# Reciprocal root mean square of blocks 1 to 8 on VectorE alone, in a fused attention and two-layer kernel

## The chip, the cores and the metric

The kernel runs on one core of a Trainium2 chip. The metric is the device time of one execution in microseconds; a lower time is better. Five engines of the core matter here: PE (TensorE, matrix products, with PEld for its weight loads), ACT (ScalarE), DVE (VectorE), POOL (GpSimd) and SP (SyncE, which only issues transfers). Each works through its own list of instructions in order, and they wait for each other through semaphores.

## The reference, cut to what matters

```python
x = attention(q, k, v)                      # chunks of 64, then 4608 rows of 512
rms = np.sqrt(np.mean(x * x, axis=-1, keepdims=True) + 1e-06)
xn = x / rms * rms_g
g = xn @ w_gate
silu = g * (1.0 / (1.0 + np.exp(-g)))
x = (silu * (xn @ w_val)) @ w_out           # 512 -> 1536 -> 512
h = x @ w_in                                # 512 -> 2048
y = (h * np.clip(h + 3.0, 0.0, 6.0) / 6.0) @ w_out2
```

The change touches the second line: one over `rms` for each of the 4608 rows.

## The kernel before

The 4608 rows are worked in nine blocks of 512. A block lies with its 512 features across partitions (four tiles of 128) and its 512 rows along the free dimension. Block 0 is normalised in a start-up stage that the change leaves alone. Then PE runs the first layer: blocks 0 to 2 one after the other (a gate product, a value product and a down product for each of twelve pieces, lines L1023 and L1048 to L1051), then blocks 3 to 8 in pairs with a scheme of seven products for eight (`product`, L1034). The second layer follows in the last half and has none of the changed code.

While PE works on the matrices of one block, the attention of later blocks and their normalisation are slipped in between. An agenda holds, for each tick (two or three slots of matrix products), the steps that are issued then: `at(t, fn, turn=...)`, and inside a tick the steps go by their turn. Each engine keeps the order in which its instructions were issued. So the place of a step is set by the agenda, and an engine that waits for a step holds up all that stands behind it.

The class `Rms` does the normalisation of blocks 1 to 8, one object for each block, in five steps of turn 1:

- `halve` (L957, L958) splits the 128 x 512 sums of squares in two parts;
- `mean` (L962, L963) multiplies both by a matrix of ones into bank `ATT` of the PSUM tensor `PS`, so that all 128 partitions hold the sum of squares of each row; ScalarE then takes the square root (L965) into the SBUF tile `rt`;
- `inv` transposes `rt` by 32 x 32 blocks on VectorE (L970), so that 16 columns hold the 512 values, takes the reciprocal of those 16 columns (L971), and transposes back with a broadcast (L972);
- `norm` (L984), in two halves, multiplies the block by the gains and by `rt`.

The banks `ATT` and `ATT + 1` are also those of attention: `Pair` (blocks 2 to 4) and `Wide` (blocks 5 to 8) write their scores there (L799 and L928), read the maxima (L809, L939), transpose the probabilities (L837) and form the values (L855). Whoever writes bank `ATT` next has to wait until the sums of squares have been read from it. The agenda places the steps of blocks 5 and 7 so that `mean` comes in tick 30, and in tick 31 `inv` (turn 1) and right after it the first half of the scores of the next unit (turn 2).

Square root, SiLU (L1331, L1353) and exponential (L709, L818) need different tables on ScalarE: each change of function from one to another has an ACT_TABLE_LOAD ahead of it, which the compiler puts in. Copies, casts, squares and ReLU need none.

Other names that come up: `ah` (L1077) and `al` (L1079 on GpSimd) are the two parts of a gated activation, which the down product L1048 to L1051 reads; L1357 and L1358 are the same for the paired blocks; L1362 is VectorE's multiply or add of a product that leaves PSUM; L1444 is a ScalarE copy of such a product.

Of the kernel before, what the change touches and what calls it, by code (L numbers as in the profile page):

```python
# [10 lines left out]
F32 = mybir.dt.float32  # L11
F32R = mybir.dt.float32r
U32 = mybir.dt.uint32
AF = mybir.ActivationFunctionType
ALU = mybir.AluOpType
# [59 lines left out]
def fused_kernel(  # L75
# [13 lines left out]
    nc = tc.nc  # L89
    B, H, S, D = q.shape  # L90
    NT, DM = out.shape
# [4 lines left out]
    N = 512  # L96
# [3 lines left out]
    scale = 1.0 / float(D) ** 0.5  # L100
# [3 lines left out]
    few_p = ctx.enter_context(tc.tile_pool(name="few", bufs=2))  # L104
# [8 lines left out]
    at_p = ctx.enter_context(tc.tile_pool(name="at", bufs=1))  # L113
# [7 lines left out]
    eps = const.tile([128, 1], F32, name="eps")  # L121
# [362 lines left out]
    sqs = {}  # L484
# [16 lines left out]
    class Att:  # L501
# [117 lines left out]
        def mean(self):  # L619
            self.ms = PS[:, self.bank, 0:1]  # L620
            for a in range(KD):
                nc.tensor.matmul(
                    self.ms, self.sq[:, a * 128:(a + 1) * 128], ones[:, 0:1], start=a == 0, stop=a == KD - 1
                )
# [9 lines left out]
        def inv(self):  # L634
            nc.vector.reciprocal(self.r, self.r)
            self.dg = self.sq[:, 384:512]
            nc.vector.tensor_scalar(self.dg, ident, self.r, None, op0=ALU.mult)
# [310 lines left out]
    class Rms:  # L948
# [11 lines left out]
        def mean(self):  # L960
            ps = PS[:, ATT, :]
            nc.tensor.matmul(ps, ones_r, self.hl[:, 0, :], start=True, stop=False)  # L962
            nc.tensor.matmul(ps, ones_r, self.hl[:, 1, :], start=False, stop=True)  # L963
            self.rt = at_p.tile([128, N], F32, tag="sqs", name="rt")
            nc.scalar.activation(self.rt, ps, AF.Sqrt, scale=1.0 / DM, bias=eps)  # L965

        def inv(self):
            t = at_p.tile([128, N], F32, tag="p", name="rT")
            r = few_p.tile([128, 16], F32, tag="rc", name="rc")
            nc.vector.transpose(out=t, in_=self.rt)  # L970
            nc.vector.reciprocal(r, t.rearrange("p (j n) -> p j n", n=32)[:, :, 0])  # L971
            nc.vector.transpose(  # L972
                out=self.rt.rearrange("p (j n) -> p j n", n=32),
                in_=r.rearrange("p (j o) -> p j o", o=1).to_broadcast([128, 16, 32]),
            )
# [140 lines left out]
    with tc.manual_schedule():  # L1116
# [208 lines left out]
        for b in range(3):  # L1325
            prev, late = None, None
            hk = 0
            for f in range(FA):
                mm_up(GB, whole(W["gate", f]), xs)
                s = sg_p.tile([128, N], F32, tag="sg", name="sg")  # L1330
# [33 lines left out]
        for p in range(3):  # L1364
# [4 lines left out]
            def gt(f, z):  # L1369
                key = ("x", 0) if z == 0 and f < 4 else (z, f // 2)  # L1370
                if key not in g:
                    g[key] = (
                        xn_p.tile([128, KD, N], F32, tag="XL", name="ge")
                        if key == ("x", 0)
                        else wp.tile([128, 2, N], F32, tag="w", name="gu")
                    )
                return g[key][:, f % 4 if key == ("x", 0) else f % 2, :]
# [6 lines left out]
            for i in range(NI + 1):  # L1384
# [13 lines left out]
                for n, (pr, m) in enumerate(slots):  # L1398
# [19 lines left out]
                    elif (pr, m) == (3, 0):  # L1418
                        t = gt(h0, 1)
                        vec(t, t, bank(4, 0), ALU.add)  # L1420
                        later = t
                    elif (pr, m) == (4, 1):
                        t = gt(h1, 0)
# [3 lines left out]
                    elif (pr, m) == (3, 1):  # L1427
                        s = hold.pop("s2")
                        vec(s, s, bank(4, 1), ALU.add)
                        t = gt(h0, 1)  # L1430
# [8 lines left out]
                    elif (pr, m) == (2, 1):  # L1439
                        t = gt(f0, 0)  # L1440
                        vec(t, t, bank(0, 1), ALU.mult)
                    elif (pr, m) == (7, 0):
                        t = gt(f1, 1)
# [3 lines left out]
                    elif (pr, m) == (7, 1):  # L1447
# [3 lines left out]
                        t = gt(f1, 1)  # L1451
# [70 lines left out]
        for n, f in enumerate(fs):  # L1522
            bank = 6 + n % 2
            i, m, z = f // 4, f // 2 % 2, f % 2
# [5 lines left out]
            s = sg_p.tile([128, N], F32, tag="sg", name="sg")  # L1530
# [24 lines left out]
        def slot(i, name):  # L1555

            key = (i, name)
            if key not in G:
                if i < 2 and name != "t":
                    t = xn_p.tile([128, KD, N], F32, tag=("XH", "XL")[i], name="gx")  # L1560
                    names = ("11", "12", "21", "22")
                elif name == "t":
                    t = wp.tile([128, 2, N], F32, tag="w", name="gt")
                    names = ()
                else:
                    t = wp.tile([128, 2, N], F32, tag="w", name="gu")
                    names = ("11", "12") if name[0] == "1" else ("21", "22")
                for n, x in enumerate(names):
                    G[i, x] = t[:, n, :]
                if not names:  # L1570
                    for n in range(2):
                        G[i - i % 2 + n, "t"] = t[:, n, :]
            return G[key]
# [81 lines left out]
        for b in range(1, NB, 2):  # L1655
# [7 lines left out]
            for I in range(NG + 1):  # L1663
# [7 lines left out]
                for pr, m in slots:  # L1671
# [20 lines left out]
                    elif pr == 3:  # L1692
                        t = slot(i, "12")
# [7 lines left out]
                    elif pr == 7:  # L1701
                        t = slot(i, "22")
# [124 lines left out]
```

## Time and profile before

| what | value |
|---|---|
| time before, median of 3 runs | 1680.77 us (1678.62 to 1683.74) |
| time of the profiled execution | 1679.51 us |
| its span, first to last instruction | 1677.7 us |
| granted TensorE clock, mean | 0.995 |
| PE busy | 1649.2 us (98%) |
| DVE busy | 1086.8 us (65%) |
| ACT busy | 845.2 us (50%) |
| POOL busy | 459.5 us (27%) |

The profiled execution took 1.8 us more than its span, which lies before the first and after the last instruction, and 1.26 us less than the median. Busy shares are shares of the span. Matrix products are pipelined, so a busy PE may still run more slowly than it could; the idle time before an instruction, and what ended it, is the safer reading.

### The profile page before, as it was taken

The numbers are of one execution on the slowest core, as the hardware profiler recorded it, in microseconds if no ns is written. First come the engines' busy times: TensorE is split into PE (matmuls) and PEld (weight loads), VectorE is DVE, ScalarE is ACT, GpSimd is POOL, SyncE is SP. The second block draws the span as 40 slices with busy tenths as digits, with TensorE's granted clock in tenths as the row PEclk, the third lists the DMA queues.
The fourth block names the chain that finished last, engine by engine and source line by source line (L and its number), as shares of the span: only waits on it lengthen the run. The fifth ranks groups of instructions, "written<-read, shape, count | busy, mean of one in ns | idle before, by whom it ended". The sixth has DMA issues, their size and how long they took to land.

```text
span 1677.7 us, 26541 instructions
## 1 busy us (share of the span) xinstructions
PE 1649.2 (98%) x9920; PEld 1350.7 (81%) x9920; DVE 1086.8 (65%) x1600; ACT 845.2 (50%) x1409; POOL 459.5 (27%) x336
## 2 busy tenths in 40 slices
PE   8999999999999999999999999999999999999998
PEld 7777888878878888788887888888788878887886
DVE  6998566656575775758436378448746764874475
ACT  6786344455454454645434344455445544654552
POOL 1001434321326522364226622131023003301310
PEclk8999999999999999999999999999999999999999
DMA  9913777747876488855979766667767786777665
GB/s 301 271 37 71 207 208 222 205 152 251 292 262 224 168 297 286 290 176 185 361 238 316 293 239 226 213 190 250 219 209 224 209 243 191 223 218 235 189 200 150
DMA packets 336096, 375.07 MB, mean 224 GB/s; under 512 B 184288, under 2 KB 260064, under 8 KB 335840
## 3 DMA queue, kind: packets, MB, share of 16 engines
q1 hardware_dynamic: 273984, 302.84, 58.4%
q10 hardware_dynamic: 61984, 70.53, 12.2%
q8 instruction: 79, 1.29, 0.3%
q14 instruction: 49, 0.40, 0.1%
HBM read 292.55 MB, written 80.74 MB: 223 GB/s over the span
## 4 chain that ended last, share of the span: by engine, by line
PE 45%; DVE 5%; DMA 1%; ACT 1%; issue 1%; SPq 1%; DVEq 0%; POOL 0%; ACTq 0%; POOLq 0%
PE PS L1034 24%; PE PS L1584 13%; PE PS L1023 2%; DVE gs L1578 1%; PE PS L1051 1%; PE PS L1048 1%; PE PS L1049 1%; DVE gt L1720 1%; PE PS L1056 1%; PE PS L1057 1%; PE PS L1060 1%; SPq L1603 1%; DMA stash_in<-sc 1%; PE PS L1784 1%; DVE oq L1598 0%
## 5 line engine op out<-in xcount | busy, mean ns | idle before, releaser
L1034 PE MATMUL PS<-xu,wo 128*128 128x512 f32 x1512 | 353.1, 392 | 3.4 <-DVE gu L1362 2.3
L1034 PEld LDWEIGHTS PS<-xu,wo 128*128 128x128 f32 x1512 | 282.3, 188 | 65.0 <-DVE gu L1362 3.1
L1034 PE MATMUL PS<-xo,wq 128*128 128x512 f32 x1344 | 305.3, 389 | 0.0
L1584 PE MATMUL PS<-gs,wq 128*128 128x512 f32 x1296 | 296.2, 390 | 2.4 <-DVE gs L1578 2.0
L1034 PEld LDWEIGHTS PS<-xo,wq 128*128 128x128 f32 x1344 | 252.3, 188 | 52.4
L1584 PEld LDWEIGHTS PS<-gs,wq 128*128 128x128 f32 x1296 | 242.7, 188 | 55.3 <-DVE gs L1578 5.0
L1023 PE MATMUL PS<-XH,w 128*128 128x512 f32 x576 | 148.9, 401 | 5.1 <-ACT sg L1331 3.1
L1023 PEld LDWEIGHTS PS<-XH,w 128*128 128x128 f32 x576 | 108.0, 191 | 29.2 <-ACT sg L1331 3.8
L1048 PE MATMUL PS<-gs,wd 128*128 128x512 f32 x288 | 113.4, 394 | 1.6 <-DVE gu L1362 1.6
L1049 PE MATMUL PS<-gs,wd 128*128 128x512 f32 x288 | 112.2, 390 | 0.0
L1079 POOL TENSOR_TENSOR al<-sg,ah 128x512 fp32r<-128x512 f32 x40 | 56.2, 1404 | 156.2 <-ACT ah L1077 151.9
L1358 POOL TENSOR_TENSOR gs<-gu,gs 128x512 fp32r<-128x512 f32 x60 | 86.6, 1461 | 42.7 <-ACT gs L1357 33.9
L1651 POOL TENSOR_TENSOR gt<-gx 128x512 f32<-128x512 f32 x8 | 10.3, 1289 | 299.8 <-DVE gx L1648 299.8
L1362 DVE TENSOR_TENSOR gu<-gu,PS 128x512 f32<-128x512 f32 x60 | 41.0, 685 | 77.4 <-ACT gu L1444 42.0
L1578 DVE TENSOR_TENSOR gs<-gu,gs 128x512 fp32r<-128x512 f32 x88 | 67.9, 792 | 31.4 <-ACT gs L1577 31.1
L1577 ACT CAST gs<-gt 128x512 fp32r<-128x512 f32 x96 | 58.3, 623 | 49.6 <-DVE gt L1720 44.3
L1515 DVE SCALAR_TENSOR_TENSOR gu<-gu,PS 128x512 f32<-128x512 f32 x48 | 32.8, 684 | 72.6 <-ACT gu L1512 72.6
L1023 PE MATMUL PS<-XL,w 128*128 128x512 f32 x288 | 78.9, 396 | 0.0
L1077 ACT CAST ah<-sg 128x512 fp32r<-128x512 f32 x52 | 32.3, 621 | 88.9 <-DVE sg L1335 63.2
L1051 PE MATMUL PS<-gs,wd 128*128 128x512 f32 x288 | 77.0, 389 | 0.0
L1577 ACT CAST gs<-gu 128x512 fp32r<-128x512 f32 x96 | 57.2, 621 | 22.8 <-DVE gs L1578 15.6
L1651 POOL TENSOR_TENSOR gt<-gu 128x512 f32<-128x512 f32 x24 | 32.5, 1355 | 129.0 <-DVE gu L1648 124.9
(251 smaller groups left out, 2887.6 us busy)
## 6 DMA issues: line engine op xcount, KB each, us to landing
wq<-stash_in SPq DMA_DIRECT2D x128, 512.0 KB
wo<-ops SPq DMA_DIRECT2D x126, 512.0 KB
wq<-sums_out SPq DMA_DIRECT2D x64, 512.0 KB
wq<-stash_out SPq DMA_DIRECT2D x48, 512.0 KB
wd<-keep_out SPq DMA_DIRECT2D x36, 512.0 KB
yd<-yst SPq DMA_DIRECT2D x18, 512.0 KB
ops<-w ACTq DMA_DIRECT2D x36, 256.0 KB
v<-in_v_dram SPq DMA_DIRECT2D x32, 256.0 KB
```

The lines of the kernel that those rows point to most:

```text
L1023: nc.tensor.matmul(ps, w(wi, c), xs[c][xi], start=(i == 0), stop=(i == n - 1))
L1034: nc.tensor.matmul(PS[:, bank, :], op[:, wi, c * 128:(c + 1) * 128], x[xi][:, c, :], start=first and i == 0, stop=last and i == 5, skip_gr ...
L1048: nc.tensor.matmul(ps, wm[0], a[0], start=first, stop=False)
L1049: nc.tensor.matmul(ps, wm[1], a[0], start=False, stop=False)
L1051: nc.tensor.matmul(PS[:, banks[m], :], w[:, 0, m * 128:(m + 1) * 128], a[1], start=False, stop=last)
L1079: nc.gpsimd.tensor_tensor(lo, t, hi.bitcast(F32), op=ALU.subtract)
L1358: nc.gpsimd.tensor_tensor(w[:, 1, :], t, w[:, 0, :].bitcast(F32), op=ALU.subtract)
L1362: nc.vector.tensor_tensor(o, x, y, op=op)
L1577: nc.scalar.copy(w[:, 0, :], x)
L1578: e.tensor_tensor(w[:, 1, :], x, w[:, 0, :].bitcast(F32), op=ALU.subtract)
L1584: nc.tensor.matmul(PS[:, banks[m], :], op[:, wi, m * 128:(m + 1) * 128], x[xi], start=first and (wi, xi) == (0, 0), stop=False, skip_group ...
L1651: nc.gpsimd.tensor_tensor(slot(i, "t"), slot(i, "12"), slot(i, "11"), op=ALU.subtract)
```

## The change

ScalarE no longer takes a square root in `mean`. `inv` transposes the sums of squares out of PSUM directly, and VectorE computes one over the root on the 16 columns by itself: the mean plus 1e-6 (`m`), a first value from the bits of `m` by one multiply-add on them read as integers, and three Newton steps of three operations each. `m` and `s` lie in unused columns of the transposed tile `t`. Code behind it moves down by nine lines (L1362 becomes L1371, and so on). The agenda is the same.

```diff
             nc.tensor.matmul(ps, ones_r, self.hl[:, 1, :], start=False, stop=True)
-            self.rt = at_p.tile([128, N], F32, tag="sqs", name="rt")
-            nc.scalar.activation(self.rt, ps, AF.Sqrt, scale=1.0 / DM, bias=eps)
+            self.ps = ps
 
         def inv(self):
             t = at_p.tile([128, N], F32, tag="p", name="rT")
-            r = few_p.tile([128, 16], F32, tag="rc", name="rc")
-            nc.vector.transpose(out=t, in_=self.rt)
-            nc.vector.reciprocal(r, t.rearrange("p (j n) -> p j n", n=32)[:, :, 0])
+            self.rt = at_p.tile([128, N], F32, tag="sqs", name="rt")
+            r, m, s = few_p.tile([128, 16], F32, tag="rc", name="rc"), t[:, 1:17], t[:, 33:49]
+            nc.vector.transpose(out=t, in_=self.ps)
+            nc.vector.tensor_scalar(
+                m, t.rearrange("p (j n) -> p j n", n=32)[:, :, 0], 1.0 / DM, 1e-6, op0=ALU.mult, op1=ALU.add
+            )
+            nc.vector.tensor_scalar(
+                r.bitcast(U32), m.bitcast(U32), -0.5, float(0x5F375A86), op0=ALU.mult, op1=ALU.add
+            )
+            for _ in range(3):
+                nc.vector.tensor_tensor(s, r, r, op=ALU.mult)
+                nc.vector.scalar_tensor_tensor(out=s, in0=s, scalar=-0.5, in1=m, op0=ALU.mult, op1=ALU.mult)
+                nc.vector.scalar_tensor_tensor(out=r, in0=s, scalar=1.5, in1=r, op0=ALU.add, op1=ALU.mult)
             nc.vector.transpose(
```

On VectorE, in the normalisation of block 5 (`kT` is the key of the next attention unit, `gu` an activation of the running pair, `rT` the tile `t`, `rc` the tile `r`), the list before was:

```order
L908 STREAM_TRANSPOSE kT<-k 128x2x8x64 [waits DMAHW5_49]
L262 SCALAR_TENSOR_TENSOR sc<-sraw,sc 128x512 [waits DMAHW6_49,DVE_49]
L265 SCALAR_TENSOR_TENSOR sraw<-sraw,sc 128x512 [waits DVE_49]
L1362 TENSOR_TENSOR gu<-gu,PS 128x512 [waits DMAHW0_49,Activation_49]
L970 STREAM_TRANSPOSE rT<-rt 128x512 [waits PE_49]
L971 RECIPROCAL rc<-rT 128x16 [waits DVE_49]
L972 STREAM_TRANSPOSE rt<-rc 128x512 [waits DVE_49]
L939 TENSOR_REDUCE mx<-PS 128x4x2 [waits PE_49]
```

and it is now, at the same place:

```order
L1371 TENSOR_TENSOR gu<-gu,PS 128x512 [waits DMAHW0_49,Activation_49]
L970 STREAM_TRANSPOSE rT<-PS 128x512 [waits PE_49]
L971 TENSOR_SCALAR rT<-rT 128x16 [waits DVE_49]
L974 TENSOR_SCALAR rc<-rT 128x16 [waits DVE_49]
L978 TENSOR_TENSOR rT<-rc 128x16 [waits DVE_49]
L979 SCALAR_TENSOR_TENSOR rT<-rT 128x16 [waits DVE_49]
L980 SCALAR_TENSOR_TENSOR rc<-rT,rc 128x16 [waits DVE_49]
...
L981 STREAM_TRANSPOSE rt<-rc 128x512 [waits DVE_49]
L939 TENSOR_REDUCE mx<-PS 128x4x2 [waits PE_49]
```

The three rows L978 to L980 stand there three times; eleven small operations, each waiting for the one before, have taken the place of one, and the first transposition, which still stands behind the add into `gu`, now reads PSUM.

On PE, from the sums of block 5 to the next scores (`sqh` are the split sums, `xu` and `wo` the operands of the running pair), the list before was:

```order
L963 MATMUL PS<-sqh,ones_r 128x512 [waits DVE_49]
L1034 MATMUL PS<-xu,wo 128x512 [waits DMAHW5_49]
L1034 MATMUL PS<-xu,wo 128x512 x5
L1034 MATMUL PS<-xu,wo 128x512 [waits DMAHW7_49,Activation_49]
...
L928 MATMUL PS<-kT,qT 64x64 [waits DVE_49,Activation_49]
```

and now:

```order
L963 MATMUL PS<-sqh,ones_r 128x512 [waits DVE_49]
L1043 MATMUL PS<-xu,wo 128x512 [waits DMAHW5_49]
L1043 MATMUL PS<-xu,wo 128x512 x5
L1043 MATMUL PS<-xu,wo 128x512 [waits DMAHW7_49,Activation_49]
...
L928 MATMUL PS<-kT,qT 64x64 [waits DVE_49]
```

Nothing moved in PE's list, but the scores no longer wait for ScalarE's square root: the bank is free once VectorE's transposition L970 has read it, and the count of VectorE's semaphore that they wait for is now that of L970 (in blocks 5 and 7, and likewise for L799 in blocks 2 and 3); before it was that of the transposed key (L908, L780).

On ScalarE, behind the same sums, the list before was:

```order
L1436 COPY s_4987<-PS 128x512 [waits PE_49,Pool_49]
L965 ACT_TABLE_LOAD
L965 ACTIVATE rt<-PS,eps 128x512 [waits PE_49]
...
L277 CAST sc<-sraw 128x512 [waits DVE_49]
L1353 ACT_TABLE_LOAD [waits DMAHW2_49]
L1353 ACTIVATE gu<-PS 128x512 [waits PE_49]
L1444 COPY gu<-PS 128x512 [waits PE_49]
```

and now:

```order
L1445 COPY s_5023<-PS 128x512 [waits PE_49,Pool_49]
...
L277 CAST sc<-sraw 128x512 [waits DVE_49]
L1362 ACTIVATE gu<-PS 128x512 [waits DMAHW2_49,PE_49]
L1453 COPY gu<-PS 128x512 [waits PE_49]
```

The square root, its table load and the load back to SiLU are gone (two issues of a store, which stand between them in both, are left out here). Over the whole program there are 39 table loads where there were 52.

## Rows read from the trace of the kernel before

**Rows 1.** Page, part 1: busy us (share of the span) and instructions.

```profile
PE 1649.2 (98%) x9920; PEld 1350.7 (81%) x9920; DVE 1086.8 (65%) x1600; ACT 845.2 (50%) x1409; POOL 459.5 (27%) x336
```

**Rows 2.** Groups by line on ACT: busy us, mean ns | idle before.

```profile
L965 ACT ACT_TABLE_LOAD x8 | 10.3, 1283 | 0.1
```

**Rows 3.** Groups by line on DVE: busy us, mean ns | idle before.

```profile
L732 DVE TENSOR_TENSOR sqs<-pT 128x128 f32<-128x128 f32 x4 | 1.2, 292 | 0.1
```

**Rows 4.** Line L824: durations in ns, min/median/max; first and last start.

```profile
L824 DVE TENSOR_SCALAR sm<-sm x14: 174/176/1219, 169.9 to 742.7; 128x16 f32<-128x16 f32 x14
```

**Rows 5.** Timeline at one L824: start us, us, engine, instruction, [idle <- releaser].

```profile
703.31 1.31 POOL L278 TENSOR_TENSOR slo<-sraw,sc 128x512 fp32r<-128x512 f32 x1 [1.78 <-ACT sc L277]
703.45 1.20 DVE L824 TENSOR_SCALAR sm<-sm 128x16 f32<-128x16 f32 x1
```

**Rows 6.** Timeline, block 5.

```profile
477.72 1.16 PE L928 MATMUL PS<-kT,qT 32*64 32x64 f32 x64 [0.69 <-DVE kT L908]
...
478.81 4.42 PE L1034 MATMUL PS<-xu,wo 128*128 128x512 f32 x18
...
479.52 1.28 ACT L1353 ACT_TABLE_LOAD   x1
...
481.92 0.69 DVE L1362 TENSOR_TENSOR gu<-gu,PS 128x512 f32<-128x512 f32 x1 [3.10 <-ACT gu L1444]
...
485.49 0.80 PE L1034 MATMUL PS<-xu,wo 128*128 128x512 f32 x1 [2.26 <-DVE gu L1362]
```

**Rows 7.** Windows behind it: us, busy by engine, then PEclk, DMA share, GB/s.

```profile
486.00:490.00 4.00, 4.00 (x72) 2.87 (x71) 2.66 (x4) 0.00 (x0) 1.66 (x1) 0.67 0.89 315
```

**Rows 8.** Timeline, block 7.

```profile
682.35 1.16 PE L928 MATMUL PS<-kT,qT 32*64 32x64 f32 x64
...
683.66 0.58 ACT L1444 COPY gu<-PS 128x512 f32<-128x512 f32 x1
```

**Rows 9.** Timeline, block 8.

```profile
772.02 1.47 POOL L1358 TENSOR_TENSOR gs<-gu,gs 128x512 fp32r<-128x512 f32 x1
...
772.26 0.70 DVE L970 STREAM_TRANSPOSE rT<-rt 128x512 f32<-128x512 f32 x1
...
772.99 0.26 DVE L971 RECIPROCAL rc<-rT 128x16 f32<-128x16 f32 x1
...
783.71 1.75 POOL L1358 TENSOR_TENSOR gs<-gu,gs 128x512 fp32r<-128x512 f32 x1 [2.53 <-DVE xt L1252]
...
785.63 1.09 PE L1051 MATMUL PS<-gs,wd 128*128 128x512 f32 x4
```

**Rows 10.** Timeline, block 1.

```profile
147.98 0.71 DVE L970 STREAM_TRANSPOSE rT<-rt 128x512 f32<-128x512 f32 x1 [1.31 <-ACT rt L965]
...
154.86 0.19 PEld L1048 LDWEIGHTS PS<-ah,w 128*128 128x128 f32 x1 [0.29 <-ACT ah L1077]
```

**Rows 11.** Timeline, block 2.

```profile
227.85 1.28 POOL L1079 TENSOR_TENSOR al<-sg,ah 128x512 fp32r<-128x512 f32 x1 [4.09 <-ACT ah L1077]
...
229.92 1.22 DVE L809 TENSOR_REDUCE mx<-PS 128x16 f32<-128x1024 f32 x1 [1.21 <-PE PS L799]
...
240.73 2.22 POOL L831 TENSOR_TENSOR p<-p,rs 128x1024 f32<-128x1024 f32 x1 [0.55 <-DMA k<-in_k_dram]
...
243.52 1.03 PE L837 MATMUL PS<-ident,p 128*128 128x128 f32 x8
```

**Rows 12.** Timeline, block 3.

```profile
299.72 0.69 DVE L1335 TENSOR_TENSOR sg<-sg,PS 128x512 f32<-128x512 f32 x1 [1.68 <-PE PS L1023]
```

**Rows 13.** Timeline, block 4.

```profile
367.29 0.71 DVE L970 STREAM_TRANSPOSE rT<-rt 128x512 f32<-128x512 f32 x1 [2.69 <-ACT rt L965]
...
375.01 0.69 DVE L1335 TENSOR_TENSOR sg<-sg,PS 128x512 f32<-128x512 f32 x1 [0.62 <-ACT sg L1331]
...
376.41 0.50 PE L1048 MATMUL PS<-ah,w 128*128 128x512 f32 x1 [1.20 <-ACT ah L1077]
```

**Rows 14.** Timeline, block 6.

```profile
565.54 0.69 ACT L965 ACTIVATE rt<-PS,eps 128x512 f32<-128x512 f32 x1 [1.93 <-PE PS L963]
```

## The prediction

> **What bounds the kernel now.** I read the page's busy shares first, then the idle time in front of PE's instructions near the eight places where a block is normalised. PE is busy for 1649.2 of 1677.7 us [rows 1], so the change can gain at most what PE idles at these places, and it loses whatever it makes PE wait. The reader should see three kinds of place in the timelines: places where PE waits already and VectorE or ScalarE ends the wait [rows 6, 13], places where PE starts just as the other engine is done, so that any delay there shows at once [rows 9, 10], and places with slack [rows 11, 12]. VectorE's 65% is an average and says nothing here: what counts is whether it has idle time between the transposition and the next operation that PE needs.
>
> **What goes from ScalarE.** Eight square roots and thirteen table loads go, eight of the loads ahead of the roots at 1.28 us each [rows 2]. ScalarE gets about 17 us from the loads alone, of which PE sees only what lies in a chain that ends in a PE wait. That is so in block 5 (the load back to SiLU at 479.52 is followed by the copy and the add that both PE and the transposition depend on [rows 6]) and in block 4 (VectorE idles 0.62 us for the SiLU behind such a load [rows 13]). The Trainium skill, page "ScalarE: Activation LUTs", section "What ACT_TABLE_LOAD costs", adds a drain of about 1.38 us to each load. The row speaks against it: from the end of the load at 480.80 to L1362 at 481.92 lie 1.12 us, in which an ACTIVATE and a copy of 0.58 us ran [rows 6, 8]. With the rule's 2.66 us the estimate for block 5 below would be some 1.4 us lower, and the sum 1686.1; I go by the row.
>
> **What VectorE gets.** One reciprocal on 16 columns took 0.26 us, with 0.03 us ahead of it [rows 9]. Eleven operations on 16 columns take its place. The trace has no TENSOR_TENSOR or SCALAR_TENSOR_TENSOR this small; the bounds are a TENSOR_SCALAR on 16 columns, 0.176 us [rows 4], and a TENSOR_TENSOR on 128 columns, 0.292 us [rows 3]. With the gap of 0.03 that is 11 x 0.21 = 2.3 us to 11 x 0.325 = 3.6 us. I take 0.18 + 0.035, since 16 columns are nearest to the first row: 2.37 us, less the 0.29 us that goes, so **+2.08 us on VectorE for each block** (+2.0 to +3.3). The transposition that now reads PSUM is taken at the 0.70 us of the one that read SBUF; multiplies with an operand in PSUM show 0.69 us [rows 6, 12].
>
> A second price comes from GpSimd. The same 16-column TENSOR_SCALAR took 1.20 us where it began 0.14 us after a GpSimd operation, and ended when that did [rows 5]; alone it takes 0.18 [rows 4]. So a GpSimd operation that starts in the 2.4 us of the chain costs up to 1.0 us more, once. For the operations with two SBUF inputs, nine of the eleven, no row of this size shows it. The Trainium skill, page "SBUF — State Buffer", section "Who interferes with whom", states it for them too: a VectorE operation with two SBUF inputs and a GpSimd operation that reads SBUF exclude each other, and who starts first holds the port. Without such a lock the sum below would be 1685.2; with it, it is 1687.5.
>
> **Block by block**, as delays of PE (minus is a gain):
>
> - Block 1: VectorE idled 1.31 us in front of the transposition, for ScalarE's root [rows 10]. Now it need not. 2.08 - 1.31 = 0.77, and as adjacent operations overlap a little, **+0.7**. PE's weight load at 154.86 already waits for `ah` [rows 10], and VectorE works without a break up to the multiply before it, so PE sees all of it.
> - Block 2: VectorE was free at 229.92 - 1.21 = 228.71. It now ends 2.08 later, plus 1.0 for the GpSimd operation that starts at 227.85 inside the chain: 231.8, against a start of L809 at 229.92, so 1.87 late. Reduction, subtraction, exponential, sum and GpSimd's L831 follow in a chain; L831 ended at 242.95, PE's L837 began at 243.52, 0.57 of slack [rows 11]. **+1.3** (without the lock +0.3).
> - Block 3: **0**. VectorE idles 1.68 us before its next multiply, waiting for PE [rows 12], and it also no longer waits for the root. Without that cover it would be up to 2.
> - Block 4: VectorE idled 2.69 us for the root, and that goes; GpSimd's cast difference now falls into the chain (+1.0). 2.08 + 1.0 - 2.69 = +0.4 at most, and the 0.62 us for the SiLU's table load goes as well [rows 13]. **-0.3** (from -1.2, PE's whole wait, to +0.4).
> - Block 5: here the scores L928 must now wait for the transposition, which stands behind the add L1362. That add ended at 482.61; without the table load of 1.28 us it ends at 481.33, and the transposition, overlapping it by 0.08, at 481.95. L928 starts at 481.97 and not at 477.72, 4.25 late [rows 6]. PE's next stretch then ends at 478.81 + 4.42 + 4.25 = 487.48, its next product could start at 487.34, and it began at 485.49 before, after 2.26 us of idle time: **+1.85**. VectorE's add for that product, 485.44 before, comes at 485.44 - 1.28 + 2.08 = 486.24, in time. One long wait has replaced two short ones. Behind the old wait PE's clock was granted at 0.67 for 4 us [rows 7], that is at 1.2 instead of 2.4 GHz for part of them; I assume the same behind the new one, no gain and no loss. 4 us at 0.67 cost 1.3 us, so if it does not fall, this block comes out near 0.5.
> - Block 6: ScalarE's root kept it waiting 1.93 us [rows 14], and VectorE's transposition stands behind two operations that depend on what follows the root. 2.08 - 1.93: **+0.15** (to +1.2 with a lock).
> - Block 7: as in block 5, without a late operand. The copy L1444 needs the product just ahead of L928, ready about 682.4; copy 0.58, add 0.69 and transposition 0.70, with 0.03 between and 0.08 of overlap, end at 684.35 [rows 6, 8]. L928 starts **+2.0** late.
> - Block 8: the transposition starts as before. Its first small operation starts at 772.99 and finds GpSimd busy until 773.49, 0.36 more than its own 0.18. 2.08 + 0.36 = 2.44; behind it VectorE, ScalarE's casts and GpSimd follow each other without a break to the operand that ends at 785.46, and PE takes it at 785.63: 0.17 of slack [rows 9]. **+2.3**.
>
> Sum: 0.7 + 1.3 + 0 - 0.3 + 1.85 + 0.15 + 2.0 + 2.3 = +8.0 us. On the profiled execution's 1679.51 us that is 1687.5; that execution lay 1.26 us under the median of the runs shown, so against the median of 1680.77 I forecast **1688.8 us**, 0.48% slower. About 0.3% (5.0 us) is what a measurement of this kernel can tell from no change.
>
> **The rivals.**
>
> - ScalarE's relief decides (not slower). Suppose the scores do not have to wait, because the transposition is done when they are due (by 477.6 in block 5, by 682.3 in block 7). Then block 5 gains: its add at 485.44 comes 1.28 earlier, 2.08 later by the chain, 0.8 late, less the slow clock if the wait is split; blocks 5 and 7 fall to +0.8 and 0, and with VectorE's rest hidden in blocks 1, 2 and 8 block 4's -0.3 is all else: 1681.3. For it speaks that PE waits for ScalarE's and VectorE's products there; against it the order: the transposition stands behind an add that waits for a product just finished. Chance 0.07.
> - VectorE's time is hidden or smaller. If the eleven operations cost little more than the reciprocal, or blocks 1, 2, 6 and 8 have more slack than I read, only the two held scores and block 4 remain: 1.85 + 2.0 - 0.3, 1684.3, within 0.3%. For it: idle time of 1.2 and 1.7 us in blocks 2 and 3 [rows 11, 12]; against it: no operation on 16 columns below 0.174 us [rows 4]. Chance 0.2.
> - The clock falls in block 7 too. Its wait of 2.0 us is near the 2.26 us behind which the clock fell in block 5 [rows 6, 7]. As there, 1.3 us; with block 5's longer wait perhaps 0.4 more: 1690.5. Chance 0.13.
> - GpSimd gets between the small operations more than once, two or three times 1.0 us in blocks 6 and 8: 1691.3. Chance 0.05.
>
> **How the numbers follow.** My forecast has 0.55. The likeliest time is the sum. Its own range is 1685.5 to 1691: block 2 and 6 without or with locks, block 4 at its ends, block 5 at 0.5. From the hidden case (1684.3, with some room) to the clock case the whole range is 1682.8 to 1692.8; the full 3.3 us for each chain would lie beyond. Slower by over 0.3% means over 1685.8: most of the forecast, the clock and the lock cases, 0.70. Within 0.3%: the hidden case, part of the first rival and the forecast's lower edge, 0.25. Faster: 0.05.
>
> **What would show it.** In the changed profile: 39 table loads on ScalarE; small operations of about 0.18 us, the chain about 2.4 us from first to last, and one of over 1 us in blocks 2 and 4; PE idle for 4 to 5 us before L928 in block 5, ended by VectorE, no wait behind it at the next product, and some 2 us before L928 in block 7; PE waiting about 2 us in block 8 for GpSimd's or ScalarE's operand. The prediction is wrong if those scores start without a wait, if the chain takes under 1 us, or if PE's idle time grows somewhere that is none of these places.

## The result, and the profile after

The changed kernel took 1691.06 us (median of 4 runs, 1689.99 to 1693.42), the kernel before 1679.69 us in the runs beside it (1677.72 to 1683.74). The ratio is 1.0065, with a 95% interval of 1.0048 to 1.0081: 11.4 us slower, where 8.0 were forecast. The profiled execution took 1690.71 us, 11.2 more than that of before.

The page of the changed kernel, part 1, answers to [rows 1]:

```profile
PE 1650.3 (98%) x9920; PEld 1351.3 (80%) x9920; DVE 1105.2 (65%) x1680; ACT 822.8 (49%) x1388; POOL 458.6 (27%) x336
```

VectorE has 80 instructions and 18.4 us more (2.3 us for each block), ScalarE 21 instructions and 22.4 us less. PE is busy only 1.1 us longer, so nearly all that was lost is idle time. All 9920 products stand in the same order in both traces, so product by product the start after minus the start before shows where PE fell behind. This is that difference, taken ahead of and behind each block's normalisation (us; "210" is one place ahead of block 2, "other" the start-up, the end and what lies between; block 3 shows no delay and has no column):

| | block 1 | 210 | 2 | 4 | 5 | 6 | 7 | 8 | other | sum |
|---|---|---|---|---|---|---|---|---|---|---|
| forecast | +0.7 | 0 | +1.3 | -0.3 | +1.85 | +0.15 | +2.0 | +2.3 | 0 | +8.0 |
| changed kernel | +0.6 | +1.2 | +2.7 | -0.5 | +2.2 | +0.1 | +3.4 | +2.5 | -1.1 | 11.2 |

Block by block the forecast holds but for three places: block 2, block 7, and a wait at 210 us that was in no term. First the held scores, which came as forecast. In the timeline of blocks 5 and 7 (compare [rows 6, 8]) L928 waits for the transposition, and behind it there is no second wait:

```profile
483.89 0.69 DVE L1371 TENSOR_TENSOR gu<-gu,PS 128x512 f32<-128x512 f32 x1 [1.68 <-ACT gu L1453]
484.49 0.71 DVE L970 STREAM_TRANSPOSE rT<-PS 128x512 f32<-128x512 f32 x1
...
485.26 1.99 PE L928 MATMUL PS<-kT,qT 32*64 32x64 f32 x64 [4.83 <-DVE rT L970]
487.17 7.02 PE L1043 MATMUL PS<-xu,wo 128*128 128x512 f32 x24
...
690.20 1.16 PE L928 MATMUL PS<-kT,qT 32*64 32x64 f32 x64 [2.02 <-DVE rT L970]
691.29 7.35 PE L1043 MATMUL PS<-xu,wo 128*128 128x512 f32 x24
```

Block 7's 3.4 us are 2.0 of wait and 1.4 of clock. The 24 products behind L928 took 7.35 us here and 7.02 in block 5. In a run further down, where the clock stayed up, the same 24 of block 5 took 5.73. The windows say it directly (us, PE busy, then PEclk; [rows 7] for before):

```profile
487.00:494.00 7.00, 7.00 (x36) 0.79 0.71 244
691.00:698.00 7.00, 7.00 (x48) 0.76 1.05 320
```

In block 8 three short waits of PE answer to the single start of [rows 9]:

```profile
788.06 0.50 PE L1057 MATMUL PS<-gs,wd 128*128 128x512 f32 x1 [0.50 <-ACT gs L1366]
...
791.01 1.20 PE L1060 MATMUL PS<-gs,wd 128*128 128x512 f32 x4 [0.83 <-POOL gs L1367]
...
795.21 0.50 PE L1057 MATMUL PS<-gs,wd 128*128 128x512 f32 x1 [0.28 <-ACT gs L1366]
```

Block 2 lost twice what was forecast (2.7 us in place of 1.3). Its timeline (compare [rows 11]):

```profile
228.69 0.18 DVE L971 TENSOR_SCALAR rT<-rT 128x16 f32<-128x16 f32 x1
228.82 1.28 POOL L1088 TENSOR_TENSOR al<-sg,ah 128x512 fp32r<-128x512 f32 x1 [4.26 <-ACT ah L1086]
228.90 1.24 DVE L974 TENSOR_SCALAR rc<-rT 128x16 uint32<-128x16 uint32 x1
230.17 0.18 DVE L978 TENSOR_TENSOR rT<-rc 128x16 f32<-128x16 f32 x1
...
233.93 1.23 DVE L815 TENSOR_TENSOR p<-PS,mx 128x1024 f32<-128x1024 f32 x1
...
235.25 1.28 ACT L818 ACT_TABLE_LOAD   x1 [6.57 <-DVE p L815]
236.54 1.06 ACT L818 ACTIVATE p<-p 128x1024 f32<-128x1024 f32 x1
...
240.60 2.11 PE L1032 MATMUL PS<-XH,w 128*128 128x512 f32 x8 [1.38 <-ACT sg L1340]
...
247.10 1.09 PE L837 MATMUL PS<-ident,p 128*128 128x128 f32 x8 [0.76 <-POOL p L831]
```

The small operations take 0.18 us each, and the one that began 0.08 us after a GpSimd operation took 1.24 and ended with it, as forecast. But the exponential's table load now runs behind the wait for L815. Before, it ran ahead of that wait, as the same place in the kernel before shows:

```profile
228.03 1.28 ACT L818 ACT_TABLE_LOAD   x1 [0.33 <-issue]
...
232.43 1.06 ACT L818 ACTIVATE p<-p 128x1024 f32<-128x1024 f32 x1 [3.11 <-DVE p L815]
```

The lists of instructions tell why. Before, the load waited for nothing, and the exponential for VectorE alone, as the root ahead of it on ScalarE had already waited for PE's mean. With the root gone, the exponential has more than one wait, and they stand on the load:

```text
before   L818 ACT_TABLE_LOAD
         L818 ACTIVATE p<-p 128x1024 [waits DVE_49]
changed  L818 ACT_TABLE_LOAD [waits DVE_49,PE_49]
         L818 ACTIVATE p<-p 128x1024 [waits Activation_49]
```

PE met the late exponential ahead of the place that the forecast had in mind. On ScalarE a SiLU stands behind the exponential, and PE waits 1.38 us for it at 240.60, where it had not waited before. With the load ahead again, in two runs further down, it waits 0.32 us (table ahead) and 0.03 us (copy) there. The wait at L837, the forecast's place, is 0.74 to 0.79 us in all three.

The load ends at 236.53 and the exponential starts 0.01 us later. The Trainium skill, page "ScalarE: Activation LUTs", section "What ACT_TABLE_LOAD costs", counts a drain of about 1.38 us with each load; this pair, like the one in the prediction, shows none behind it.

The third surprise lies between the chains of blocks 1 and 2, far from both: PE waited 1.65 us at 211.27 (0.43 before) for a SiLU whose table load stands behind stores on ScalarE's queue, and one of these waited for a transfer to land.

```profile
209.33 1.28 ACT L1340 ACT_TABLE_LOAD   x1 [6.75 <-DMA ops<-oh]
...
211.27 0.96 PE L1032 MATMUL PS<-XH,w 128*128 128x512 f32 x3 [1.65 <-ACT sg L1340]
```

### The profile page after: what moved, and what is told of

Same layout as the page of the kernel before. It is cut to its first block, busy times and chain, and to the rows that moved or that the text cites. A ratio compares the mean times of both kernels' runs of the same rounds, so it can differ in the third digit from the quotient of the medians.

```text
span 1688.9 us, 26593 instructions
## 1 busy us (share of the span) xinstructions
PE 1650.3 (98%) x9920; PEld 1351.3 (80%) x9920; DVE 1105.2 (65%) x1680; ACT 822.8 (49%) x1388; POOL 458.6 (27%) x336
## 4 chain that ended last, share of the span: by engine, by line
PE 46%; DVE 5%; DMA 1%; issue 1%; SPq 0%; ACT 0%; DVEq 0%; POOL 0%; ACTq 0%; POOLq 0%
PE PS L1043 23%; PE PS L1593 13%; PE PS L1032 3%; DVE gs L1587 1%; PE PS L1060 1%; PE PS L1057 1%; PE PS L1058 1%; PE PS L1065 1%; PE PS L1066 1%; PE PS L1069 1%; DVE gt L1729 1%; DVE oq L1607 1%; DMA stash_in<-sc 1%; PE PS L1793 1%; SPq L1612 0%
## 5 line engine op out<-in xcount | busy, mean ns | idle before, releaser
L1371 DVE TENSOR_TENSOR gu<-gu,PS 128x512 f32<-128x512 f32 x60 | 41.0, 685 | 76.8 <-ACT gu L1453 36.6
```

The lines of the kernel that those rows point to most:

```text
L1371: nc.vector.tensor_tensor(o, x, y, op=op)
```

## The experiments

The table gives PE's delay against the kernel before by place, as above, in each run's profiled execution. The text gives the medians and intervals of the timed runs.

| run | block 1 | 210 | 2 | 4 | 5 | 6 | 7 | 8 | other | sum |
|---|---|---|---|---|---|---|---|---|---|---|
| copy | +0.6 | -0.1 | +1.3 | -0.2 | +0.5 | +3.2 | -0.2 | +2.3 | +1.1 | 8.5 |
| hold | +0.1 | 0.0 | 0.0 | +0.1 | +3.2 | +0.2 | +5.7 | -0.3 | -0.9 | 8.1 |
| one step | -0.2 | +2.3 | +1.5 | -1.5 | +1.6 | -0.5 | +3.3 | +0.9 | +1.3 | 8.7 |
| table ahead | +0.6 | -0.1 | +1.6 | -0.4 | +1.7 | +0.8 | +4.9 | +1.9 | +0.9 | 11.9 |
| early | -0.1 | +1.9 | +2.5 | -0.5 | +1.0 | +0.7 | +0.1 | +2.0 | +0.5 | 8.0 |
| late | -0.2 | +0.8 | +2.5 | -0.5 | -2.1 | +0.9 | +3.5 | +3.4 | +1.1 | 9.4 |
| late, block 2 mended | -0.2 | +1.0 | +0.3 | -0.4 | -2.0 | +1.9 | +2.4 | +3.4 | +4.9 | 11.2 |
| that, two steps | -0.2 | +1.6 | 0.0 | -1.1 | -0.7 | +0.9 | +3.3 | +0.7 | +1.2 | 5.7 |
| blocks 4 and 5 | 0.0 | +0.6 | 0.0 | -0.4 | -0.5 | +0.2 | +0.1 | -0.2 | +3.3 | 2.9 |
| that, two steps | 0.0 | +0.1 | 0.0 | -1.1 | +0.8 | +0.5 | +0.1 | -0.5 | -0.8 | -1.0 |
| block 1 alone | -0.2 | +0.4 | 0.0 | 0.0 | -1.5 | +0.2 | +0.1 | -0.3 | -1.4 | -2.7 |
| all, two steps | -0.2 | +0.7 | 0.0 | -1.1 | -0.7 | -0.6 | 0.0 | +1.3 | +0.8 | 0.4 |

**Copy: ScalarE frees the bank.**

```diff
-            self.ps = ps
+            self.rt = at_p.tile([128, N], F32, tag="sqs", name="rt")
+            nc.scalar.copy(self.rt, ps)
...
-            nc.vector.transpose(out=t, in_=self.ps)
+            nc.vector.transpose(out=t, in_=self.rt)
```

> The changed kernel, but ScalarE copies the mean from its PSUM bank to SBUF (a plain copy of 0.6 us, no root, no table load) and VectorE transposes that copy, so the bank ATT comes free without VectorE; all eleven small operations stay. Theory (the held scores of blocks 5 and 7 carry half of the loss): no wait at L928; block 5 falls from +2.2 to +0.8, block 7 from +3.4 to 0; and the wait for TensorE moves back onto the copy, so that the exponential's table load of block 2 runs ahead again, 1.3 us: 1691.1 - 4.8 - 1.3 = 1685.0, up to 1686.5 if the copy keeps VectorE waiting in blocks 4 and 6. Rival (the scores' wait only stands in for the wait at the next product, and VectorE's small operations carry the loss in every block): PE waits as long in blocks 5 and 7, at the product behind, and only block 2 gains: 1689.8.

1688.08 us, ratio 1.0043 (1.0029 to 1.0056). Blocks 5, 7 and 2 came as the theory says (+0.5, -0.2, +1.3): the held scores are gone, and the table load is ahead again. The total lies between the two sides, because block 6 lost 3.2, which neither expected. There the copy waits 3.21 us for PE's mean, and L255, which VectorE's next operations need, stands behind it on ScalarE:

```profile
566.78 0.59 ACT L965 COPY rt<-PS 128x512 f32<-128x512 f32 x1 [3.21 <-PE PS L963]
567.27 0.66 ACT L255 ACTIVATE sc<-sraw 128x512 f32<-128x512 f32 x1
...
569.56 0.53 DVE L971 TENSOR_SCALAR rT<-rT 128x16 f32<-128x16 f32 x1
570.13 1.20 DVE L974 TENSOR_SCALAR rc<-rT 128x16 uint32<-128x16 uint32 x1
```

In the changed kernel L255 runs at 567.80, ahead of the end of the mean at 571.1. So the change also has a gain here, which the copy gives back: ScalarE no longer waits for PE in the middle of block 6. About 2 us of the copy's loss stand under "other": at 670.00 PE waits 1.36 us for a SiLU behind ScalarE's stores, one of which waited for a transfer, as at 210.

**Hold: the bank alone.** The kernel before, in which VectorE also reads the bank, for one column.

```diff
+            self.ps = ps
             nc.scalar.activation(self.rt, ps, AF.Sqrt, scale=1.0 / DM, bias=eps)
...
+            nc.vector.tensor_copy(few_p.tile([128, 1], F32, tag="hd", name="hold"), self.ps[:, 0:1])
             nc.vector.transpose(out=t, in_=self.rt)
```

> The kernel before, with its square roots and table loads, plus one VectorE copy of a single column out of the bank ATT just ahead of the transposition (0.1 to 0.2 us): VectorE then holds the bank as in the changed kernel, without the small operations. Theory: the scores L928 wait for the add L1362 and this copy: block 5 about 5.0 us late where 2.26 us of waiting behind it goes, +2.65; block 7 from 682.35 to about 685.2, +2.8; 1679.7 + 5.5 = 1685.2, and 1687.8 if the clock falls behind both waits. Rival (the bank is not what costs; the chain of small operations is): no more than the eight copies, under 1 us: 1680.5.

1690.29 us, ratio 1.0056 (1.0037 to 1.0076). One column, eight times, costs nearly as much as the whole change:

```profile
481.63 0.15 DVE L971 COPY hold<-PS 128x1 f32<-128x1 f32 x1
481.93 1.98 PE L928 MATMUL PS<-kT,qT 32*64 32x64 f32 x64 [5.77 <-DVE hold L971]
483.84 7.09 PE L1036 MATMUL PS<-xu,wo 128*128 128x512 f32 x24
...
687.78 1.74 PE L928 MATMUL PS<-kT,qT 32*64 32x64 f32 x64 [2.79 <-DVE hold L971]
689.45 7.87 PE L1036 MATMUL PS<-xu,wo 128*128 128x512 f32 x22
```

The wait of 2.79 is the 2.8 expected, and the clock fell behind both waits. The rival falls: who reads the bank, and where that reader stands in its queue, is a cost of its own. Both waits are longer than in the changed kernel (4.83 and 2.02), since the two table loads, for the root and back to SiLU, still stand ahead of the add, and in block 7 the slow clock takes more (7.87 us for 22 products). The profiled execution, 1687.72 us, is the fastest of the five and agrees with the 1687.8 expected for a clock that falls; what adds 2.5 us in the median stays open.

**One step.** `for _ in range(1)` in place of 3.

> The changed kernel with one Newton step in place of three, so that the reciprocal root is less exact: six small operations, about 1.27 us of VectorE, fewer in each block. Theory (the chain shows only in blocks 1, 2 and 8, the held scores of blocks 5 and 7 wait for the transposition ahead of it): block 1 -0.7, block 2 -1.3, block 8 -1.3, blocks 4 and 6 up to -0.4 each, blocks 3, 5 and 7 nothing: 1691.1 - 3.5 = 1687.6. Rival (the chain shows in every block): 8 x 1.27 = 10 us less, 1681. Rival (the chain is hidden nearly everywhere, the bank and the tables carry all): under 1 us less, 1690.5.

1688.62 us, ratio 1.0046 (1.0029 to 1.0064). That is 2.4 less than the changed kernel, but the two intervals overlap, so the places tell more than the total; this profile also had 1.1 us more at 210 and 1.5 at the end of the kernel. Against the changed kernel's row the blocks give -0.8 (1), -1.1 (2), -1.1 (4), -0.6 (5), -0.65 (6), -0.1 (7) and -1.6 (8). The theory's blocks 1, 2, 7 and 8 are right; 4 gained more than the 0.4 allowed, and 5 and 6 a little.

**Table ahead.** In block 2, behind the mean:

```diff
+            if self.blk == 2:
+                nc.scalar.activation(few_p.tile([128, 1], F32, tag="wm", name="warm"), ps[:, 0:1], AF.Exp)
```

> The changed kernel plus, in block 2 alone, one exponential of a single column on ScalarE right behind the mean, whose only use is that the exponential's table is loaded there, some 9 us ahead of the exponential L818, and not behind its wait. Theory (in block 2 the table load of 1.28 us moved behind the wait for VectorE's subtraction, since the root no longer carried the wait for TensorE): L818 starts 1.28 us earlier relative to L815, block 2 costs +1.3 instead of +2.6: 1689.8. Rival (the extra 1.3 us of block 2 come from GpSimd's lock and later operations; the load would be hidden): L837 starts as late as in the changed kernel, 1691.1.

1691.94 us, ratio 1.0073 (1.0052 to 1.0093): the total does not show it. In the profiled execution block 7 took 1.5 us more than in the changed kernel's, which hides the gain there; why the median shows none is open. The place does show it: block 2 fell from 2.7 to 1.6, and L818 followed L815 without a load between them.

```profile
223.34 1.28 ACT L966 ACT_TABLE_LOAD   x1
224.64 0.17 ACT L966 ACTIVATE warm<-PS 128x1 f32<-128x1 f32 x1
...
232.99 1.22 DVE L815 TENSOR_TENSOR p<-PS,mx 128x1024 f32<-128x1024 f32 x1
...
234.31 1.06 ACT L818 ACTIVATE p<-p 128x1024 f32<-128x1024 f32 x1 [6.56 <-DVE p L815]
```

**Early: the transposition behind the mean.**

```diff
-            self.ps = ps
+            self.t = at_p.tile([128, N], F32, tag="p", name="rT")
+            nc.vector.transpose(out=self.t, in_=ps)
...
-            nc.vector.transpose(out=t, in_=self.ps)
```

> The changed kernel with one move: the transposition out of the bank ATT is issued right behind the mean (in the agenda's tick of the mean), so that on VectorE it stands ahead of the add of blocks 5 and 7 on which it waited; the small operations stay where they are. Theory (the scores wait for the place of the transposition in VectorE's order, not for ScalarE or for a transfer): no wait over 0.5 us at L928; block 5 from +2.2 to +0.8 (the next product's add is later by the chain, less a table load), block 7 from +3.4 to about 0; but in block 6 VectorE now waits for the mean ahead of L256, which costs PE about 1 us; 1691.1 - 4.8 + 1.0 = 1687.3. Rival (it is the eleven operations, wherever they stand; the scores only meet the delay first): PE loses the same 4 to 5 us at the product behind L928, 1691.

1685.45 us, ratio 1.0038 (1.0024 to 1.0051). Block 7 is free. In block 5 a wait of 2.47 us is left, since the transposition now stands behind L262 and L265; the limit of 0.5 us was wrong there.

```profile
482.41 1.73 PE L928 MATMUL PS<-kT,qT 32*64 32x64 f32 x64 [2.47 <-DVE rT L965]
484.06 8.31 PE L1043 MATMUL PS<-xu,wo 128*128 128x512 f32 x24
```

**Late: the chain behind what PE needs.** With the early transposition, `m` kept in a tile of its own, and the agenda's ticks for `inv`:

```diff
-            (1, (-6, -5, -4, -3, -3)), (2, (20, 21, 22, 24, 25)), (3, (42, 43, 44, 46, 47)),
+            (1, (-6, -5, -4, -3, -3)), (2, (20, 21, 23, 24, 25)), (3, (42, 43, 45, 46, 47)),
...
-            ((28, 30, 31, 33, 34), (56, 58, 59, 60, 61))
+            ((28, 30, 32, 33, 34), (56, 58, 60, 60, 61))
```

> The move of the run with the early transposition, and the chain of small operations (all three Newton steps, all but the first multiply) put one tick later in blocks 2, 3, 5 and 7 and, in blocks 6 and 8, behind L262 and L265 on VectorE, just ahead of the multiplies that need its result. Theory (a chain costs only by what stands behind it in VectorE's queue): in blocks 5 and 7 the adds that PE waits for come ahead of it, and PE gains the table load of 1.28 us that block 5 no longer has; in block 8 L277 and the casts behind it are not late; blocks 1 and 2 stay (+0.7, +2.6), block 4 -0.4: 0.7 + 2.6 - 0.4 - 1.3 + 0.5 + 0 + 1.0 = +3.1 on 1679.6, 1682.7. Rival (VectorE's 2.1 us per block come out at PE sooner or later, since everything behind depends on the normalised block): as the early transposition alone, 1687.

1691.63 us, ratio 1.0075 (1.0059 to 1.0091): the total missed by 9 us. Block 5 alone did what was expected (-2.1). In block 7 the chain now stands ahead of another add that PE waits for (2.50 us at 703.05 for L1372, where it was 0.86). In block 8 PE waits 2.12 us at 790.47. Behind both waits the products started 0.43 us apart, where 0.23 is usual, so the clock fell too. In block 8 the chain was moved under GpSimd's work:

```profile
780.05 1.35 POOL L278 TENSOR_TENSOR slo<-sraw,sc 128x512 fp32r<-128x512 f32 x1 [2.03 <-ACT sc L277]
780.25 1.18 DVE L980 SCALAR_TENSOR_TENSOR rm<-rm 128x16 f32<-128x16 f32 x1
...
781.36 2.53 POOL L1368 TENSOR_TENSOR gs<-gu,gs 128x512 fp32r<-128x512 f32 x2
781.47 1.21 DVE L981 SCALAR_TENSOR_TENSOR rc<-rm,rc 128x16 f32<-128x16 f32 x1
782.71 1.21 DVE L979 TENSOR_TENSOR rm<-rc 128x16 f32<-128x16 f32 x1
```

Three GpSimd operations, three small operations of 1.2 us: the fourth rival of the prediction, brought about by the move.

**Late, with block 2 mended.** The chain of block 2 behind L815 (`turn=2.5` for its `inv`), and the table ahead.

> The run before with two edits in block 2 alone: the chain behind the subtraction L815 in VectorE's order, where VectorE waits for ScalarE's exponential anyway, and the exponential's table loaded ahead by an exponential of one column. All three Newton steps. Theory: block 2 falls from +2.6 to 0; left are block 1 (+0.7) and what block 8 keeps: 1680.2, level with the kernel before. Rival (block 2's loss is GpSimd's lock and the later multiplies, not the order): the multiplies behind the chain are late instead, 1682.5.

1690.91 us, ratio 1.0064 (1.005 to 1.0079). Block 2 fell from 2.5 to 0.3, as the theory says, but the total missed by 10.7: blocks 7 and 8 kept what the late chain costs them, and this profile's start-up was 3 us longer.

**That, with two steps.**

> The run before with two Newton steps in place of three, so that the reciprocal root is a little less exact: three small operations, 0.64 us, fewer in each block. Theory (only block 1 and block 8 still show the chain): -0.64 in block 1 and up to -0.6 in block 8, 1679.2, within what can be told from the kernel before. Rival (the chain is not seen any more): as the run before, 1680.2.

1682.76 us, ratio 1.0023 (1.0013 to 1.0033). The expected total assumed the late placing to be good; the fall of 8 us between the medians is far more than the 0.64 us a block. The profiles differ by 5.5 us: block 8 gives 2.7, where two small operations meet GpSimd and no longer three, block 6 gives 1.0, and the start-up, which the edit doesn't touch, 3.5; other places take some of it back. What the rest of the medians' fall is stays open.

**Blocks 4 and 5 alone.** The kernel before, with the early transposition and the chain in these two, block 5's one tick late.

> The kernel before, with the new reciprocal root (three Newton steps) in blocks 4 and 5 alone, where the runs so far gave PE time back: in block 4 in its old place, in block 5 the transposition behind the mean and the chain one tick later, behind the adds that PE waits for. Theory (the change gains where a table load or the root stood in a chain that ends in a wait of PE, and where the chain lies behind what PE needs): block 4 -0.4, block 5 -2.1 as in the run with the late chain, 1679.7 - 2.5 = 1677.2, faster than both kernels. Rival (the gain of block 5 came out of the delays ahead of it in that run, and is given back behind): level, 1679.7.

1678.94 us, ratio 1.0001 (0.9992 to 1.001): level. Block 4 gave its 0.4. Block 5 gave 0.5 and not 2.1, because behind the same wait of L928 (2.42 us) the clock fell, which it did not in the late run (2.40 us):

```profile
481.32 1.27 PE L928 MATMUL PS<-kT,qT 32*64 32x64 f32 x64 [2.42 <-DVE rT L967]
482.52 7.21 PE L1054 MATMUL PS<-xu,wo 128*128 128x512 f32 x24
```

In the late run the same two rows read:

```profile
481.58 1.16 PE L928 MATMUL PS<-kT,qT 32*64 32x64 f32 x64 [2.40 <-DVE rT L966]
482.67 5.73 PE L1044 MATMUL PS<-xu,wo 128*128 128x512 f32 x24
```

The clock seems to have taken the gain in most timed runs, and not in the profiled one alone: the granted clock has a mean of 0.9939 over this kernel's 11 runs and of 0.9953 over the 35 of the kernel before beside them. By an estimate from these two, their difference times the time, this kernel loses 2.3 us more to the clock, about the 2.5 us that the theory expected to gain.

**That, with two steps.**

> The run before with two Newton steps in place of three (a little less exact in these two blocks). Theory: block 4 -1.0, as its multiply is what PE waits for there; block 5 the same: 1676.6. Rival (block 4's wait ends with ScalarE, not with the chain): 1677.2.

1679.40 us, ratio 1.0007 (0.9999 to 1.0016): no difference in the total; block 4 came to -1.1, as expected, and block 5 to +0.8 with the slow clock. The mean granted clock of its 11 runs was lower still, 0.9932.

**Block 1 alone.**

> The kernel before, with the new reciprocal root (three Newton steps) in block 1 alone, the transposition behind the mean. Theory: block 1 costs 0.7 and nothing else, 1680.4; the wait of over 1 us for a transfer ahead of block 2 (PE at 210 us), which came in most runs with the change and in none without, is chance and comes or not. Rival (that wait is the change's, by block 1, where ScalarE's stores are issued earlier without the root): PE waits 1.3 to 2.3 us at 210 us here too, 1681.9.

1680.49 us, ratio 1.0007 (0.9997 to 1.0018). The 0.7 of block 1 is not there: behind the mean the transposition stands ahead of the operation that makes `al` (L1101 in this run), and block 1 comes out at -0.2; it is -0.1 or -0.2 in every run with block 1's transposition behind the mean. At 210 PE waited 0.91 us. It waited 1.06 and 0.59 in the two runs before this one, whose first three blocks are those of the kernel before (0.43), and 0.32 to 2.74 in the others. So this wait varies without a change ahead of it too, by 0.6 us; whether the change adds to it stays open.

**All eight blocks, each at its best place, two steps.**

> The new reciprocal root in all eight blocks at the best place found for each: the transposition behind the mean, the chain in its first place but in block 2 behind L815 with the exponential's table loaded ahead, and two Newton steps. Theory: block 1 0, block 2 0, block 4 -1.0, block 5 +0.5, block 6 +0.3, block 7 +0.1, block 8 +1.8 (its chain still stands ahead of what PE takes at once): 1681.4, or 1682.6 with the late transfer at 210 us. Rival (block 8 has slack against the shorter chain): 1679.7.

1679.94 us, ratio 1.0006 (0.9994 to 1.0018): level with the kernel before, and some 10 us under the changed kernel by the two ratios. What remains of the chain are block 8's waits (+1.3), 0.83 us for GpSimd's part of `gs` and 0.27 for ScalarE's. No version was measurably faster than the kernel before.

## Why the prediction was right, and where it was not

- **What bounds it.** Right in the main: PE's busy time grew by 1.1 us only, and most of the loss is idle time at the places named, plus the clock behind it. But the prediction gave idle time at any other place as a sign of being wrong, and the wait at 210 is one.
- **The chain.** 2.08 us for each block was right to 0.1: eleven operations of 0.174 to 0.18 us with 0.035 between (2.3 us measured, less 0.29). GpSimd's lock came where forecast in blocks 2 and 4 and at 0.35 in block 8; in block 6 a lock of 1.1 us came too, and stayed hidden.
- **The held scores of blocks 5 and 7.** Shown by three runs: taking the bank from VectorE's late reader (copy, early) ends the wait in block 7, and giving the old kernel such a reader (hold) makes it. In block 5 the scores started 4.15 us late (4.25 forecast), and one long wait took the place of two short ones, as forecast. That the block's total came near, +2.2 for +1.85, needed luck as well: the prediction assumed that the clock falls behind the new wait as behind the old. It did, but behind a wait of 2.40 us at the same place (late run) it did not.
- **Block 2, +1.3, measured +2.7.** The failed step. "Reduction, subtraction, exponential" took the exponential as it was; the exponential's table load moved into that chain. The step also followed the chain to L837 alone, while 1.38 us of the wait came at a SiLU behind the exponential. With the load ahead, block 2 shows 1.6 (1.3 in the copy run). That the root carried a wait for others could be read in the order of ScalarE's instructions, not in the diff.
- **Block 7, +2.0, measured +3.4.** The wait was right (2.02 us); the clock behind it was the rival with a chance of 0.13, at 1.4 us (1.3 priced).
- **The wait at 210.** In no term and no rival: 1.2 us in this profile, and 0.1 less to 2.3 more than before in the others; the cause stays open.
- **The sum.** These three add 1.4 + 1.4 + 1.2 = 4.0; other places take off 1.1, of which 0.9 is start-up. 8.0 + 4.0 - 1.1 = 10.9, against 11.2 measured. The wait at 210 and the start-up, +1.2 and -0.9, nearly cancel, which is luck. The median of 1691.06 lies just above the forecast's own range (to 1691) and inside the whole range, which takes in the clock rival.

## What to carry to other kernels

When an operation moves to another engine, look at who frees its input: a shared PSUM bank is free when its last reader is done, and a reader that stands late in its queue holds up PE, even with one column of work. Removing an instruction also removes the waits that it carried for those behind it; look at which instruction carries them now, and whether a table load that used to run ahead stands behind them. A chain of small operations costs what stands behind it in the queue and is due. Moving it back is no gain by itself: the late run put it ahead of other adds that PE waits for and under GpSimd's operations.

## What the runs showed of the hardware

- The clock behind a wait of PE of 2.2 to 2.5 us is not a fixed cost. Behind L928's wait of 2.40 us (late run) it stayed at the level of 2.4 GHz, and 24 products took 5.73 us; behind 2.42 and 2.47 us (blocks 4 and 5 alone, early run) the same 24 took 7.21 and 8.31 us, part of them at 1.2 GHz. In the run with block 1 alone the old wait of block 5 (2.28 us there) was followed by a granted clock of 1.00 where the kernel before had 0.67 [rows 7], and block 5 came out 1.5 us earlier with no change there. A difference of 1.5 us with the same code at that place (2.6 from the late to the early run) is as large as most terms of this study; whether it comes by chance or from what runs around that place, one profile of each kernel does not show. The 35 runs of the kernel before, with a granted clock of 0.993 to 0.997 and times of 1676.30 to 1684.61 us, vary without any edit. The late run's mean is 0.9915, against 0.9952 for the kernel before beside it. Estimated as for blocks 4 and 5 alone, that is 6 us of its loss. The windows on PE behind these waits, first the late run, then the early one, then block 1 alone:

```profile
482.00:490.00 8.00, 8.00 (x143) 1.00 0.76 192
```

```profile
482.00:490.00 8.00, 7.59 (x79) 0.57 0.72 234
```

```profile
484.00:490.00 6.00, 5.84 (x84) 1.00 0.94 294
```

- Operations with two SBUF inputs on only 16 columns are locked out by GpSimd too: 1.18 and 1.21 us where 0.18 is usual, one for each GpSimd operation. The Trainium skill, page "SBUF — State Buffer", section "Who interferes with whom", states this exclusive lock, and the rows of the late run agree.
